# Score tiles in pairs, and O items 13 behind H, in a fused attention and feed-forward kernel

## The chip, the core and the metric

The kernel runs on one core of a Trainium2 chip. The core has a matrix engine (TensorE, PE in the profile, with its weight loads on a row PEld), two engines for elementwise work that can read the matrix results (VectorE, DVE; ScalarE, ACT), one [...] (GpSimd, POOL), and SyncE (SP), which here only issues DMAs. Matrix results land in PSUM, eight banks of 128 x 512 float32. Everything else lives in the on-chip memory or, by DMA, in the chip's main memory. The metric is the time of one execution in microseconds (us).

## What is computed

Attention with a window of 128 keys and a linear position bias over 8 batches, 8 heads, 576 positions and head size 64, then a feed-forward layer over the 4608 tokens that come out of it:

```python
def _attn_ref(q, k, v):                      # 8 x 8 x 576 x 64
    scores = scale * np.matmul(q, k.transpose(0, 1, 3, 2))
    bias = slopes[:, None, None] * (-np.abs(rel))[None, :, :]
    mask = (rel >= 0) & (rel < 128)
    scores = np.where(mask, scores + bias[None], -1000000000.0)
    attn = softmax(scores)
    return np.matmul(attn, v)

def _moe_ref(x, w_in, w_out, beta):          # 4608 x 512, 512 x 2048, 2048 x 512
    h = x @ w_in
    g = h * (1.0 / (1.0 + np.exp(-beta * h)))
    return g @ w_out
```

## The kernel before

*Feed-forward.* The tokens are worked in 9 groups of 512. An H item (`HS(g, j)`, L356) is four matmuls of 128 x 512 into one bank `hps`; ScalarE takes a tanh of it (`sig`, L369) and VectorE makes the gate from both (`gT`, L370), which frees the bank. Two banks serve `hps`, so the H after next waits for the gT of this one. Sixteen H make a group. An O item (`OS(g, i, n)`, L374) is four matmuls (L380) that add a quarter of the sum over the 2048 features to an O tile, one of four tiles of 128 tokens in a group. With n = 3 the tile is done: ScalarE copies it out (`osb`, L395) and a DMA, mostly on POOL's queue, stores it. Two banks serve O tiles.

*Attention.* Queries and keys are loaded on SP's queue (L95), cast by POOL (L129), transposed by a DMA on SP's queue (`TD`, L248) into `QK`; values are loaded by POOL's queue (L137) from batch 3 on. A score tile (`SC(b, m, p)`, L257) holds the two heads of pair p against half the key blocks of batch b: m = 0 the blocks 0 and 1, m = 1 the blocks 2, 4 and 3. It is four or six matmuls (L277) over 64 rows, the two heads on the two halves of the array's rows, each head with a bank of its own. Its tile `sps` is two banks, and there is one such tile. From batch 2 on ScalarE then takes four exponentials (L290), two a head, and VectorE multiplies by a mask (L294), which gives `pt`; for batches 0 and 1 the bias is added by matmuls and there is one exponential. There are 8 score tiles a batch, 40 in batches 3 to 7.
A value item (`PV(b, qb, g)`, L306) is four or eight matmuls of 65 columns for one block of queries and four heads, into one of two banks tagged "t"; VectorE divides by the sum (`zs`, L326, and `xn`, L327). `X(b, qb)` brings xn into the transposed tokens `XT` that H reads: by matmuls and a copy for batches 0 to 2, by a DMA on SP's queue (L341) from batch 3 on.

*Order.* PE's order is written by hand, and around the change so are those of SP and POOL; the framework orders ScalarE and VectorE. From batch 2 on, `moe` lists the H and O items, and `merge(steps, first)` lists the attention's steps with the loads, casts and transposes set among them by step number. `spread(moe, todo, lead, goals)` goes through `moe` and lays the steps between the items, by a cost of 2 for a score tile and 1 for a PV, so that each goal (the tokens of a group, 10 items before its first H) is met. The score tiles thus stand alone, with two to five H and O items between them. O items run 10 behind H: the list `late` (10 items) of one group and `early` (6) of the next go between the H. In `early` two O tiles alternate.

The banks are: `psum_s` 2 (one score tile), `psum_t` 2 (values, transposes), `psum_h` 2, `psum_o` 2.

Of the kernel before, what the change touches and what calls it, by code (L numbers as in the profile page):

```python
# [17 lines left out]
def kernel(  # L18
# [235 lines left out]
    COLS = {0: (0, 384), 1: (128, 256), 2: (0, 384), 3: (192, 320), 4: (128, None)}  # L254
    OWN = (256, 320)

    def SC(b, m, p, pool=None, fill=0):  # L257
        qk = QK[b % 2]
        sps = (pool or psum_s).tile([P, 2, 512], F32, name="sps", tag="sps")
        idle(sps[:, 0, :], fill)  # L260
        if b < NPE:
            for e in range(2):
                nc.tensor.matmul(  # L263
                    sps[:, e, :], lhsT=sident[:, 2 * p + e, :], rhs=table[m][:],
                    start=True, stop=False, skip_group_check=True,
                )
        for kb in ((0, 1), (2, 4, 3))[m]:
            at, after = COLS[kb]
            nq = {3: P + 64, 4: 64}.get(kb, 2 * P)
            for e in range(2):  # L270
                o = sps[:, e, at : at + min(nq, 512 - at)]
                if kb in (0, 2):
                    o = bass.AP(
                        tensor=o.tensor, offset=o.offset,
                        ap=[list(o.ap[0]), [after - at, 2], [1, P]],
                    )
                nc.tensor.matmul(  # L277
                    o,
                    lhsT=qk[64 * e : 64 * e + 64, 1, p, P * kb : P * kb + P],
                    rhs=qk[64 * e : 64 * e + 64, 0, p, P * kb : P * kb + nq],  # L280
                    start=b >= NPE, stop=True, skip_group_check=True,
                )
        pt = pt_pool.tile([P, 2, 512], BF16, name="pt", tag="pt")
        if b < NPE:
            nc.scalar.activation(out=pt[:], in_=sps[:], func=ACTF.Exp, scale=qscale)  # L285
        else:
            for e in range(2):
                h = 2 * p + e
                for half, cols in ((0, slice(0, OWN[m])), (1, slice(OWN[m], 512))):
                    nc.scalar.activation(  # L290
                        out=pt[:, e, cols], in_=sps[:, e, cols], func=ACTF.Exp,
                        scale=qscale, bias=bias[:, half, h : h + 1],
                    )
            nc.vector.tensor_tensor(  # L294
                out=pt[:], in0=pt[:],
                in1=masks[m][:].rearrange("p (o c) -> p o c", o=1).broadcast_to([P, 2, 512]),
                op=ALU.mult,
            )
        pts[b, m, p] = pt
# [166 lines left out]
    def pv(b, qb, g):  # L466
        return step(lambda: PV(b, qb, g), 1)
# [43 lines left out]
    def by_pair(b):  # L511
# [5 lines left out]
            pv(b, 2, 1),  # L517
        ]

    def by_block(b):  # L520

        e = b - 1
        if e < NTE:
            r = [sc(b, 0, 0), pv(e, 3, 1), sc(b, 0, 1), x(e, 3), pv(e, 4, 1)]
        else:
            r = [sc(b, 0, 0), pv(e, 2, 1), x(e, 2), pv(e, 3, 1), x(e, 3), sc(b, 0, 1),
                 pv(e, 4, 1), x(e, 4)]
        return r + [
            sc(b, 0, 2), pv(b, 0, 0)] + ([x(e, 4)] if e < NTE else []) + [
            sc(b, 0, 3), pv(b, 1, 0), sc(b, 1, 0), pv(b, 0, 1), x(b, 0),  # L530
            sc(b, 1, 1), pv(b, 1, 1), x(b, 1), sc(b, 1, 2), pv(b, 2, 0), sc(b, 1, 3), pv(b, 3, 0),
            pv(b, 4, 0),
        ]

    with tc.manual_schedule(engines={mybir.EngineType.PE}):

        for sb in range(NQB):
            c = load_v(0, sb)()
            if sb in (1, 3):
                with tc.issue_after(c.ins):  # L540
                    for n in ((0,), (1, 2))[sb // 2]:
                        load_w1(n)
        for p in range(NP):
            c = load_pair(1, p, None if p else VS[0][0:1, NQB - 1, 0, 0:1])
            if p == 1:
                with tc.issue_after(c.ins):
                    load_w1(3)
                load_tail(1)
        for sb in range(NQB):
            c = load_v(1, sb)()  # L550
            if sb == 3:
                with tc.issue_after(c.ins):
                    for n in range(4):
                        load_w2(n)
        with tc.tile_pool(name="psum_x", bufs=2, space=bass.MemoryType.PSUM) as psum_x:
            pools = [psum_x, psum_s, psum_x]

            def sc0(m, p, fill=0):
                SC(0, m, p, pools[0], fill)
                pools.append(pools.pop(0))  # L560

            w = psum_t.tile([P, 512], F32, name="w", tag="t")
            idle(w[:], 9)
            TP(0, 0, 0)
            c = TP(0, 0, 1)
            with tc.issue_after(c.ins):
                late_consts()
            sc0(0, 0, 3)
            load_beta()
            TP(0, 1, 0)  # L570
            TP(0, 1, 1)
            sc0(0, 1, 2)
            TT(0)
            TP(0, 2, 0)
            sc0(1, 0, 1)
            TP(0, 2, 1)
            sc0(1, 1)
            TP(0, 3, 0)
            sc0(0, 2)
            TP(0, 3, 1)  # L580
            sc0(1, 2)
            PV(0, 0, 0)
            sc0(0, 3)
            PV(0, 1, 0)
            sc0(1, 3)
            for qb in (2, 3):
                PV(0, qb, 0)
        psum_h = ctx.enter_context(
            tc.tile_pool(name="psum_h", bufs=2, space=bass.MemoryType.PSUM))
        def hs(g):  # L590
            return [lambda j=j: HS(g, j) for j in range(NFF)]

        h0, s1 = hs(0), by_pair(1)
        with tc.tile_pool(name="psum_z", bufs=2, space=bass.MemoryType.PSUM) as psum_z:
            spare["z"] = psum_z
            w = psum_s.tile([P, 2, 512], F32, name="w", tag="sps")
            for qb in range(NQB - 1):
                PV(0, qb, 1, (psum_z, "ops") if qb % 2 else (psum_h, "hps"))  # L600
                idle(w[:, 0, :], 1)
                if qb:
                    X(0, qb - 1)
            X(0, NQB - 2)
            for it in [
                h0[0], pv(0, 4, 0), h0[1], pv(0, 4, 1), h0[2], h0[3], x(0, 4), h0[4], h0[5],
                s1[0], h0[6], s1[1],
            ]:
                it()
            del spare["z"]  # L610
        for p in range(NP):
            load_pair(2, p)
            if p == 1:
                load_tail(2)

        with tc.tile_pool(name="psum_y", bufs=1, space=bass.MemoryType.PSUM) as psum_y:
            spare["y"] = [psum_s, psum_y]
            spread(h0[7:14], s1[2:-1], 0, [(7, len(s1) - 3)])
            del spare["y"]
        psum_o = ctx.enter_context(  # L620
            tc.tile_pool(name="psum_o", bufs=2, space=bass.MemoryType.PSUM))
        for it in s1[-1], h0[14], pv(1, 3, 1), x(1, 2), h0[15], x(1, 3):
            it()

        s2 = by_pair(2)
        for f in s2[0:2]:
            f()
        steps, first = [pv(1, 4, 1)] + s2[2:9] + [x(1, 4)] + s2[9:] + [x(2, 2)], {}
        for b in range(NTE, B):
            first[b] = len(steps)  # L630
            steps += by_block(b)
        steps += [pv(B - 1, 2, 1), x(B - 1, 2), pv(B - 1, 3, 1), x(B - 1, 3), pv(B - 1, 4, 1),
                  x(B - 1, 4)]
        with tc.manual_schedule(engines={mybir.EngineType.SP, mybir.EngineType.Pool}):

            early = [(0, 0), (1, 0), (0, 1), (1, 1), (0, 2), (1, 2)]
            late = [(0, 3), (1, 3)] + [(i, n) for i in (2, 3) for n in range(4)]

            def os(g, order):
                return [lambda i=i, n=n: OS(g, i, n) for i, n in order]  # L640

            todo, goals = merge(steps, first), []
            moe = hs(1) + os(0, early + late) + os(1, early)
            for g in range(2, NTG):
                b, r = divmod(TOKG * (g + 1) - 1, S)
                goals.append((len(moe) - 10, todo.index(at[b, r // P]) + 1))
                o = os(g - 1, late) + (os(g, early) if g < NTG - 1 else [])
                h = hs(g)
                moe += sum(([h[n]] + o[n : n + 1] for n in range(NFF)), [])
            spread(moe, todo, 2, goals)  # L650
            while stores:
                flush()
            for it in os(NTG - 1, early + late):
                it()


# [28 lines left out]
```

## Time and profile before

| What | Value |
|---|---|
| Time, median of 6 runs | 335.56 us (333.5 to 338.3) |
| The profiled execution: time, span | 335.34 us, 333.2 us |
| L364 (H), 576 matmuls of 512 columns | 144.1 us busy |
| L380 (O), 576 matmuls of 512 columns | 142.5 us busy |
| L277 (scores), 320 matmuls | 35.7 us busy in three shapes |
| L369 tanh, x144 | 99.1 us on ScalarE, mean 691 ns |
| L290 exponentials, x192 | 75.0 us on ScalarE as a union, mean 478 ns |
| L370 gate, x144; L294 mask, x48 | 98.3 and 35.4 us on VectorE |
| DMA, 100 to 120 us; 220 to 240 us; 260 to 280 us | 187, 80 and 47 GB/s |

A row of the profile's list of groups gives line, engine, operation, what is written from what, and how often; of PE some records are missing (554 of 576 for H). The matmuls are pipelined: one of 512 columns is shown with 379 ns, yet the next begins 216 ns after it, so an item of four takes 0.86 us from its start to the next item's start. In the timeline each line is a run of instructions: start, duration, engine, line, operation, count, and in brackets the engine's idle time before it with what ended it. A row "issue" of the waits is time in which the engine waited for nothing that the profile shows.

### The profile page before, as it was taken

The numbers are of one execution on the slowest core, as the hardware profiler recorded it, in microseconds if no ns is written. First come the engines' busy times: TensorE is split into PE (matmuls) and PEld (weight loads), VectorE is DVE, ScalarE is ACT, GpSimd is POOL, SyncE is SP. The second block draws the span as 40 slices with busy tenths as digits, with TensorE's granted clock in tenths as the row PEclk, the third lists the DMA queues.
The fourth block names the chain that finished last, engine by engine and source line by source line (L and its number), as shares of the span: only waits on it lengthen the run. The fifth ranks groups of instructions, "written<-read, shape, count | busy, mean of one in ns | idle before, by whom it ended". The sixth has DMA issues, their size and how long they took to land.

```text
span 333.2 us, 6160 instructions
## 1 busy us (share of the span) xinstructions
PE 317.5 (95%) x2237; PEld 151.7 (46%) x2280; DVE 192.0 (58%) x413; ACT 215.4 (65%) x416; POOL 106.5 (32%) x173
## 2 busy tenths in 40 slices
PE   8989799999999999999999999999999999999895
PEld 3454345444544444444444444444444444444342
DVE  7658468995336675556566656566565555334500
ACT  5667684896558867777677667775776664454611
POOL 6743582163753525424242334420100010010000
PEclk9999999999999999999999999999999999999999
DMA  7999999999999999999999879990402002010011
GB/s 186 241 195 246 236 228 238 180 192 180 224 220 170 182 192 192 173 174 231 119 223 159 155 112 202 183 137 3 103 31 65 31 33 84 19 65 31 32 62 66
DMA packets 138638, 48.26 MB, mean 145 GB/s; under 512 B 125664, under 2 KB 136176, under 8 KB 138608
## 3 DMA queue, kind: packets, MB, share of 16 engines
q1 hardware_dynamic: 108208, 32.19, 53.3%
q0 software_dynamic: 30224, 15.54, 30.6%
q8 instruction: 18, 0.29, 0.4%
q10 hardware_dynamic: 176, 0.14, 0.1%
q14 instruction: 12, 0.10, 0.1%
HBM read 36.71 MB, written 9.44 MB: 138 GB/s over the span
## 4 chain that ended last, share of the span: by engine, by line
PE 84%; DMA 6%; DVE 3%; SPq 2%; POOL 2%; issue 1%; ACT 1%
PE ops L380 37%; PE hps L364 34%; PE sps L277 5%; DMA fst<-in_k_dram 5%; PE pv L321 3%; PE pv L317 2%; DMA fst<-in_v_dram 2%; SPq L109 1%; DVE gT L370 1%; PE tps L224 1%; ACT sig L369 1%; PE sps L263 1%; DVE xn L327 1%; POOL W L188 1%; DVE pt L294 1%
## 5 line engine op out<-in xcount | busy, mean ns | idle before, releaser
L364 PE MATMUL hps<-XT,W 128*128 128x512 bf16 x554 | 144.1, 379 | 3.4 <-DVE gT L370 1.5
L369 ACT ACTIVATE sig<-hps,beta_h 128x512 bf16<-128x512 f32 x144 | 99.1, 691 | 72.7 <-PE hps L364 66.3
L380 PE MATMUL ops<-W,gT 128*128 128x512 bf16 x558 | 142.5, 379 | 1.2 <-issue 0.3
L370 DVE SCALAR_TENSOR_TENSOR gT<-sig,hps 128x512 bf16<-128x512 bf16 x144 | 98.3, 684 | 56.4 <-ACT sig L369 55.7
L290 ACT ACTIVATE pt<-sps,bias 128x256 bf16<-128x256 f32 (+1 forms) x192 | 75.0, 478 | 11.0 <-PE sps L277 11.0
L364 PEld LDWEIGHTS <-W 128*128 128x128 bf16 x576 | 52.0, 98 | 58.8 <-issue 5.6
L380 PEld LDWEIGHTS <-gT 128*128 128x128 bf16 x576 | 51.2, 97 | 55.7 <-issue 2.1
L294 DVE TENSOR_TENSOR pt<-pt,mask 128x1024 bf16<-128x1024 bf16 x48 | 35.4, 737 | 42.9 <-ACT pt L290 42.9
L398 POOL DMA_DIRECT2D out_dram<-osb x32 | 17.9, 560 | 110.5 <-ACT osb L395 110.5
L129 POOL CAST bst<-fst 128x512 bf16<-128x512 f32 (+1 forms) x50 | 32.0, 644 | 57.8 <-DMA fst<-in_q_dram 37.9
L327 DVE TENSOR_TENSOR xn<-pv,zs 128x256 bf16<-128x256 f32 (+1 forms) x80 | 33.7, 422 | 2.4
L395 ACT ACTIVATE osb<-ops 128x512 f32<-128x512 f32 x35 | 21.0, 601 | 18.1 <-PE ops L380 18.0
L321 PE MATMUL pv<-vs,pt 128*128 128x65 bf16 x320 | 28.7, 193 | 1.5 <-DVE qkT L243 0.5
L321 PEld LDWEIGHTS <-pt 128*128 128x128 bf16 x320 | 21.7, 97 | 11.2 <-DVE qkT L243 0.7
L277 PE MATMUL sps<-qkT 64*128 64x256 bf16 (+2 forms) x320 | 25.2, 252 | 0.1
L317 PE MATMUL pv<-vs,pt 128*128 128x65 bf16 x256 | 24.0, 193 | 0.7 <-DVE XT L350 0.5
L326 DVE RECIPROCAL zs<-pv 128x4 f32<-128x4 f32 (+1 forms) x80 | 14.1, 176 | 16.5 <-PE pv L321 16.2
L317 PEld LDWEIGHTS <-pt 128*128 128x128 bf16 x256 | 19.9, 98 | 7.5 <-issue 1.0
L277 PEld LDWEIGHTS <-qkT 64*128 64x128 bf16 x320 | 10.4, 94 | 27.5 <-issue 24.2
L137 POOL DMA_DIRECT2D vs<-in_v_dram x25 | 21.4, 859 | 1.0 <-issue 0.5
L285 ACT ACTIVATE pt<-sps 128x1024 bf16<-128x1024 f32 x16 | 16.3, 1023 | 6.5 <-PE sps L277 5.8
L113 POOL CAST bst<-fst 128x512 bf16<-128x512 f32 x24 | 14.6, 621 | 18.4 <-DMA fst<-in_q_dram 11.4
(49 smaller groups left out, 109.5 us busy)
## 6 DMA issues: line engine op xcount, KB each, us to landing
fst<-in_q_dram SPq DMA_DIRECT2D x32, 256.0 KB, 4.6
fst<-in_k_dram SPq DMA_DIRECT2D x32, 256.0 KB, 5.1
out_dram<-osb POOLq DMA_DIRECT2D x32, 256.0 KB, 3.1
fst<-in_v_dram SPq DMA_DIRECT2D x12, 256.0 KB, 7.2
vs<-in_v_dram POOLq DMA_DIRECT2D x20, 128.0 KB, 5.5
W<-in_moe_w_in_dram POOLq DMA_DIRECT2D x4, 512.0 KB, 7.2
W<-in_moe_w_out_dram POOLq DMA_DIRECT2D x4, 512.0 KB, 15.3
fst<-in_q_dram SPq DMA_DIRECT2D x8, 128.0 KB, 5.4
```

Of the source, the lines that this page charges most:

```text
L129: nc.gpsimd.tensor_copy(out=t[0 : ROWS[sb], i], in_=f)
L137: nc.gpsimd.dma_start(out=to, in_=v[b, :, P * sb : P * sb + ROWS[sb], :].rearrange("h p d -> p h d"))
L277: nc.tensor.matmul(o, lhsT=qk[64 * e : 64 * e + 64, 1, p, P * kb : P * kb + P], rhs=qk[64 * e : 64 * e + 64, 0, p, P * kb : P * kb + nq], ...
L290: nc.scalar.activation(out=pt[:, e, cols], in_=sps[:, e, cols], func=ACTF.Exp, scale=qscale, bias=bias[:, half, h : h + 1],)
L294: nc.vector.tensor_tensor(out=pt[:], in0=pt[:], in1=masks[m][:].rearrange("p (o c) -> p o c", o=1).broadcast_to([P, 2, 512]), op=ALU.mult,)
L317: nc.tensor.matmul(pv[:, hl, 0 : D + 1], lhsT=weights(b, qb - 1, h, 1), rhs=vs[:, qb - 1, h, 0 : D + 1], start=True, stop=False,)
L321: nc.tensor.matmul(pv[:, hl, 0 : D + 1], lhsT=weights(b, qb, h, 0), rhs=vs[:, qb, h, 0 : D + 1], start=qb == 0, stop=True,)
L327: nc.vector.tensor_tensor(out=xn[0:nq, 4 * g : 4 * g + 4, :], in0=pv[0:nq, :, 0:D], in1=zs[0:nq].broadcast_to([nq, 4, D]), op=ALU.mult,)
L364: nc.tensor.matmul(hps[:], lhsT=W1[:, c, bass.ts(j, P)], rhs=XT[:, c, c0 : c0 + TOKG], start=(c == 0), stop=(c == NDM - 1),)
L369: nc.scalar.activation(out=sig[:], in_=hps[:], func=ACTF.Tanh, scale=beta_h[:, j : j + 1])
L370: nc.vector.scalar_tensor_tensor(out=gts[g][:, j, :], in0=sig[:], scalar=1.0, in1=hps[:], op0=ALU.add, op1=ALU.mult)
L380: nc.tensor.matmul(ops_[:], lhsT=gT[:, j, i * P : i * P + P], rhs=W2[:, j, :], start=(j == 0), stop=(j == NFF - 1),)
```

## The change

- In batches 3 to 7 score tiles are issued two at a time (`visit`). The first keeps the two banks of `psum_s`. The second, `split=True`, has its heads in two single banks: one of the O tiles' pool and one of the value pool.
- A pair stands at the start of each stretch of eight H and O items, between the H that follows an O tile's last item and the next O tile's first. The steps of the batch are cut into stretches at the pairs, and `spread` lays each stretch's steps among its own eight items. Two more stretches without a pair (`pause`) hold the end of batch 7.
- O items run 13 behind H and tile by tile: `early` and `late` are replaced by one order, (0,0), (0,1), (0,2), (0,3), (1,0) and so on. The stretch before the first pair has 28 items, the next two 4 and 6.
- `PV(b, 3, 0)` and `PV(b, 4, 0)` move from the end of their batch behind the first pairs of the next one, and the second halves of block 2 of batch 2 too.

The attention's steps then advance by one batch in 32 items.

```diff
-    def SC(b, m, p, pool=None, fill=0):
+    def SC(b, m, p, pool=None, fill=0, split=False):
         qk = QK[b % 2]
-        sps = (pool or psum_s).tile([P, 2, 512], F32, name="sps", tag="sps")
-        idle(sps[:, 0, :], fill)
+        if split:
+
+            sps = [
+                psum_o.tile([P, 512], F32, name="sps0", tag="ops")[:],
+                psum_t.tile([P, 512], F32, name="sps1", tag="t")[:],
+            ]
+        else:
+            both = (pool or psum_s).tile([P, 2, 512], F32, name="sps", tag="sps")
+            sps = [both[:, e, :] for e in range(2)]
+        idle(sps[0], fill)
...
+    visits = []
+
+    def visit(b, m, p):
+        def f():
+            SC(b, m, p)
+            SC(b, m, p + 1, split=True)
+
+        visits.append(f)
+        return [f, lambda: None]
+
+    def pause():
+        visits.append(lambda: None)
+        return [visits[-1]]
+
     def by_block(b):
 
         e = b - 1
         if e < NTE:
-            r = [sc(b, 0, 0), pv(e, 3, 1), sc(b, 0, 1), x(e, 3), pv(e, 4, 1)]
+            r = [pv(e, 2, 1), pv(e, 3, 1), x(e, 2), x(e, 3)], [pv(e, 4, 1), x(e, 4)]
         else:
-            r = [sc(b, 0, 0), pv(e, 2, 1), x(e, 2), pv(e, 3, 1), x(e, 3), sc(b, 0, 1),
-                 pv(e, 4, 1), x(e, 4)]
-        return r + [
-            sc(b, 0, 2), pv(b, 0, 0)] + ([x(e, 4)] if e < NTE else []) + [
-            sc(b, 0, 3), pv(b, 1, 0), sc(b, 1, 0), pv(b, 0, 1), x(b, 0),
-            sc(b, 1, 1), pv(b, 1, 1), x(b, 1), sc(b, 1, 2), pv(b, 2, 0), sc(b, 1, 3), pv(b, 3, 0),
-            pv(b, 4, 0),
-        ]
+            r = [pv(e, 2, 1), x(e, 2), pv(e, 3, 0), pv(e, 3, 1), x(e, 3)], [
+                pv(e, 4, 0), pv(e, 4, 1), x(e, 4)]
+        return (
+            visit(b, 0, 0) + r[0] + visit(b, 0, 2) + r[1]
+            + visit(b, 1, 0) + [pv(b, 0, 0), pv(b, 0, 1), x(b, 0)]
+            + visit(b, 1, 2) + [pv(b, 1, 0), pv(b, 1, 1), x(b, 1), pv(b, 2, 0)]
+        )
...
-            early = [(0, 0), (1, 0), (0, 1), (1, 1), (0, 2), (1, 2)]
-            late = [(0, 3), (1, 3)] + [(i, n) for i in (2, 3) for n in range(4)]
+
+            order = [(i, n) for i in range(4) for n in range(4)]
...
-            todo, goals = merge(steps, first), []
-            moe = hs(1) + os(0, early + late) + os(1, early)
+            todo = [[]]
+            for f in merge(steps, first):
+                if f in visits:
+                    todo.append([])
+                todo[-1].append(f)
+            moe = [hs(1) + os(0, order[0:12]), os(0, order[12:]), os(1, order[0:3])]
             for g in range(2, NTG):
-                b, r = divmod(TOKG * (g + 1) - 1, S)
-                goals.append((len(moe) - 10, todo.index(at[b, r // P]) + 1))
-                o = os(g - 1, late) + (os(g, early) if g < NTG - 1 else [])
-                h = hs(g)
-                moe += sum(([h[n]] + o[n : n + 1] for n in range(NFF)), [])
-            spread(moe, todo, 2, goals)
+                o = os(g - 1, order[3:]) + (os(g, order[0:3]) if g < NTG - 1 else [])
+                for j, h in enumerate(hs(g)):
+                    moe[-1].append(h)
+                    if j % 4 == 1:
+                        moe.append([])
+                    moe[-1] += o[j : j + 1]
+            for n, m in enumerate(moe):
+                r = todo[n] if n < len(todo) else []
+                if n and r:
+                    r.pop(0)()
+                spread(m, r, 2 if n == 0 else 1, [(len(m) - (n == 0), len(r))])
             while stores:
                 flush()
-            for it in os(NTG - 1, early + late):
+            for it in os(NTG - 1, order):
                 it()
```

More of the change, by code (lines that the diff above doesn't have):

```diff
@@ L263, in SC @@
                 nc.tensor.matmul(
-                    sps[:, e, :], lhsT=sident[:, 2 * p + e, :], rhs=table[m][:],
+                    sps[e], lhsT=sident[:, 2 * p + e, :], rhs=table[m][:],
                     start=True, stop=False, skip_group_check=True,
@@ L270, in SC @@
             for e in range(2):
-                o = sps[:, e, at : at + min(nq, 512 - at)]
+                o = sps[e][:, at : at + min(nq, 512 - at)]
                 if kb in (0, 2):
@@ L284, in SC @@
         if b < NPE:
-            nc.scalar.activation(out=pt[:], in_=sps[:], func=ACTF.Exp, scale=qscale)
+            nc.scalar.activation(out=pt[:], in_=both[:], func=ACTF.Exp, scale=qscale)
         else:
@@ L290, in SC @@
                     nc.scalar.activation(
-                        out=pt[:, e, cols], in_=sps[:, e, cols], func=ACTF.Exp,
+                        out=pt[:, e, cols], in_=sps[e][:, cols], func=ACTF.Exp,
                         scale=qscale, bias=bias[:, half, h : h + 1],
@@ L627 @@
             f()
-        steps, first = [pv(1, 4, 1)] + s2[2:9] + [x(1, 4)] + s2[9:] + [x(2, 2)], {}
+        steps, first = [pv(1, 4, 1)] + s2[2:9] + [x(1, 4)] + s2[9:-1], {}
         for b in range(NTE, B):
@@ L631 @@
             steps += by_block(b)
-        steps += [pv(B - 1, 2, 1), x(B - 1, 2), pv(B - 1, 3, 1), x(B - 1, 3), pv(B - 1, 4, 1),
-                  x(B - 1, 4)]
+        e = B - 1
+        steps += pause() + [pv(e, 2, 1), x(e, 2), pv(e, 3, 0), pv(e, 3, 1), x(e, 3)]
+        steps += pause() + [pv(e, 4, 0), pv(e, 4, 1), x(e, 4)]
         with tc.manual_schedule(engines={mybir.EngineType.SP, mybir.EngineType.Pool}):
-            early = [(0, 0), (1, 0), (0, 1), (1, 1), (0, 2), (1, 2)]
-            late = [(0, 3), (1, 3)] + [(i, n) for i in (2, 3) for n in range(4)]
+            order = [(i, n) for i in range(4) for n in range(4)]
             def os(g, order):
                 return [lambda i=i, n=n: OS(g, i, n) for i, n in order]
-            todo, goals = merge(steps, first), []
-            moe = hs(1) + os(0, early + late) + os(1, early)
-            for g in range(2, NTG):
-                b, r = divmod(TOKG * (g + 1) - 1, S)
-                goals.append((len(moe) - 10, todo.index(at[b, r // P]) + 1))
-                o = os(g - 1, late) + (os(g, early) if g < NTG - 1 else [])
-                h = hs(g)
-                moe += sum(([h[n]] + o[n : n + 1] for n in range(NFF)), [])
-            spread(moe, todo, 2, goals)
+            todo = [[]]
[4 more added lines that the diff above has]
+            moe = [hs(1) + os(0, order[0:12]), os(0, order[12:]), os(1, order[0:3])]
+            for g in range(2, NTG):
+                o = os(g - 1, order[3:]) + (os(g, order[0:3]) if g < NTG - 1 else [])
[9 more added lines that the diff above has]
+                spread(m, r, 2 if n == 0 else 1, [(len(m) - (n == 0), len(r))])
             while stores:
                 flush()
-            for it in os(NTG - 1, early + late):
+            for it in os(NTG - 1, order):
                 it()
```

## The prediction

> **What bounds the kernel now.** I read the busy table and the 40 slices first, then the waits, the timeline around one score tile, SP's queue and the end.
>
> ```profile
> PE 317.5 (95%) x2237; PEld 151.7 (46%) x2280; DVE 192.0 (58%) x413; ACT 215.4 (65%) x416; POOL 106.5 (32%) x173
> ...
> PE   8989799999999999999999999999999999999895
> ...
> DMA  7999999999999999999999879990402002010011
> ```
>
> TensorE is the bound from the sixth slice to the end; only what takes time out of its row counts. The waits of TensorE (first row: its weight loads) show where it loses any:
>
> ```profile
> PEld L277 <- issue: 24.2, 57, 0.4
> ...
> PE hps L364 <- DVE gT L370: 1.5, 2, 0.9
> ```
>
> 57 score tiles each begin with 0.4 us in which no weights are loaded, and twice an H waits for VectorE. The timeline shows both. A score tile of batch 5, m = 1:
>
> ```profile
> 172.76 1.03 PE L364 MATMUL hps<-XT,W 128*128 128x512 bf16 x4
> ...
> 173.72 0.39 PE L277 MATMUL sps<-qkT 64*128 64x256 bf16 x6
> 173.82 0.69 ACT L369 ACTIVATE sig<-hps,beta_h 128x512 bf16<-128x512 f32 x1 [1.04 <-PE hps L364]
> ...
> 174.05 1.04 PE L380 MATMUL ops<-W,gT 128*128 128x512 bf16 x4
> ...
> 174.41 1.56 ACT L290 ACTIVATE pt<-sps,bias 128x320 bf16<-128x320 f32 x4
> ...
> 174.92 1.03 PE L364 MATMUL hps<-XT,W 128*128 128x512 bf16 x4
> ...
> 175.98 0.69 ACT L369 ACTIVATE sig<-hps,beta_h 128x512 bf16<-128x512 f32 x1
> 176.00 0.69 DVE L294 TENSOR_TENSOR pt<-pt,mask 128x1024 bf16<-128x1024 bf16 x1 [0.77 <-ACT pt L290]
> ...
> 176.61 0.17 DVE L326 RECIPROCAL zs<-pv 128x4 f32<-128x4 f32 x1
> ```
>
> Elsewhere an H or O item follows the last after 0.86 us (175.91 to 176.77), so the scores could begin at 173.62; they begin at 173.72. They stream 0.23 us and O begins at 174.05, not 173.95; its successor comes after 0.87, not 0.86. A visit to the 64-row mode thus costs 0.10 + 0.09 + 0.01 = 0.20 us beside its streaming.
>
> **The change part by part.** The sum is made against the profiled execution: 335.34 us, span 333.2 and 2.1 around it, 0.2 under the median of 335.56.
>
> *Pairs.* 40 lone tiles become 20 pairs: 20 x 0.20 = 4.0 us less on TensorE, the path. Inside a tile a second set of weights costs 0.01 beyond streaming; 20 of those at the seams give back 0.2. The trace has no seam between two tiles in different banks; bounds are 0 and the whole 0.20 (nothing gained); I take 0.01, since the nearest rows, the second keys of a tile, have the same row halves and no lone drain. Gain 3.8. The Trainium skill (TensorE: Matmul & The Clock Gate, section Single matmul latency) puts the drain of a matmul that nothing follows at roughly 175 ns; with that at each change of mode, two a pair, the gain would be 20 x 0.35 = 7.0. The row's 0.10 and 0.09 are measured here, and I keep them.
>
> *The end.* Group 8, the last, now has 13 O items among its 16 H, not 10. Before, six H in a row have two hps banks, and each bank comes back 1.6 us after its H:
>
> ```profile
> 311.02 1.89 PE L364 MATMUL hps<-XT,W 128*128 128x512 bf16 x8 [0.85 <-DVE gT L370]
> ...
> 313.54 0.81 PE L364 MATMUL hps<-XT,W 128*128 128x512 bf16 x3 [0.64 <-DVE gT L370]
> ```
>
> Counted from start to start the two gaps are 1.0 and 0.8. Now three H stand together; only the third waits: 0.8. Gain 1.0. The last stores are unchanged, since the last two O tiles ran one by one before too.
>
> *The burst.* A pair issues eight exponentials at once, and the tanh of the next H stands behind them on ScalarE's queue; that H's bank is wanted by the second H after it. Times from the end of streaming of the H ahead of the pair: that H's tanh runs from 0.20 (173.62 to 173.82) and lets the next start at 0.79 (174.41); eight exponentials occupy to 0.79 + 2 x 1.57 = 3.93 for m = 1 (174.41 to 175.98 each tile), 3.65 for m = 0 (1.43 each). The next H's tanh, ready at 2.6, ends at 4.62 (4.34). On VectorE the second mask is ready at 3.95 (3.80), the zs and xn of the first PV at 3.6; the mask spaces the row by 0.61 (176.00 to 176.61), zs by 0.21, xn by 0.34, gT takes 0.68 and frees the bank 0.06 later. Meanwhile TensorE does: pair to 0.66, O 0.87, H, O, PV (0.13 or 0.24), H, O (0.86 each), in two of four pairs a second PV, then the H that wants the bank: at 5.11 after pair (1,0), written (m, first p), 5.23 after (0,2), 5.47 after (0,0) and (1,2).
> With zs, xn, mask, gT in this order for m = 1 the bank is free at 5.48 and 5.60: waits of 0.36 and 0.13; for m = 0, with the mask ahead of xn, at 5.25: about 0. Sum 0.5 a batch, 2.5 us in five. VectorE's queue isn't written out by hand, so its order is unknown: with the mask first and gT next, 0.27 a batch at the least (1.4 in all); with gT last of the four, 0.73 + 0.38 + 0.47 + 0.23 = 1.8 a batch, 9 in all. I take 2.5: at 176.00 and 176.61 the trace has mask and zs in the order in which they became ready.
> The skill speaks against the change here: TensorEngine Tiling (Array Packing), section PSUM Bottleneck, says that tiling speeds up TensorE but not the emptying of PSUM, which may become the bottleneck. By sums it doesn't: eight items and a pair take some 8.1 us of TensorE (8 x 0.86 + 0.66 + 2.5 PV), ScalarE 3.0 + 4 x 0.69 + 0.60 = 6.4. It holds only locally, as worked out.
>
> *The new banks.* The first half tile takes the O bank that the last pair left; its eight exponentials ended 4 us ago. The O tile after the pair takes the bank of the tile that ended; an H and the pair (1.5 us) cover its 0.6 us copy. Twice in batch 3 no H lies between: 0.2 each. The value bank is free for as long. These banks cost nothing while that H stands there; without it, 0.2 a pair, 4 us.
>
> *Start, and moved DMAs.* Batches 3 to 7 take some 32.5 us each now (29 to 37 before, by the tile starts 89.5, 118.6, 154.5, 192.1, 228.8), and batch 3 comes sooner. Its 10 loads, 10 key and query transposes and 5 or 6 value transposes stand on SP's queue, which has no gap from 66 to 157 us:
>
> ```profile
> 93.39 0.76 SPq L95 DMA_DIRECT2D fst<-in_k_dram  x1
> 94.26 6.20 SPq L248 DMA_TRANSPOSE qkT<-bst  x4
> 100.52 0.58 SPq L95 DMA_DIRECT2D fst<-in_q_dram  x1
> ```
>
> The second of the four, batch 3's last, is issued at 96.45 and lands 4.3 later, at 100.8. Its scores began at 104.6; now, by counting items, at about 98.3 (first pair at 87.0 and 11.3 of items): up to 2.5 us of waiting, less what earlier loads in the new list win. I take 1.5, with 0 and 3 as ends; the O waits above and a wait of the first pair for the transposes of 82.9 (landing 5.1 later) lie within it. After that a batch needs some 32 us of SP (118.8 to 151.0 from first load to first load, without a gap) against 32.5 of TensorE: just covered. POOL's casts, value loads and stores take 14 us a batch, and all keep their order; X comes 16 us or more ahead of its H but for group 3, where some 1 us is left. PV, O and H are as many as before.
>
> Sum: 335.3 - 3.8 - 1.0 + 2.5 + 1.5 = 334.5, that is 1.1 under the median.
>
> **The rivals.**
> *The cover holds* (TensorE gets the pairs whole): the burst costs 0 to 1 and the start 0 to 1. 335.3 - 4.8 + 0.5 = 331.0. For it: ScalarE at 65%, and PV counts that I took at their least. Against: the 0.3 that pair (1,0) lacks in any order.
> *The burst decides, slower*: gT placed last after each pair, 9 us: 335.3 - 4.8 + 9 + 1.5 = 341.0. It turns the sign above 3.3 us, 0.17 a pair. For it: at 177.16 gT does stand behind zs and xn though its tanh was done at 176.67. Against: there the hps bank wasn't late.
> *SP becomes the bound*: 85.5 to 118.8, loads of batch 4 to loads of batch 5, took SP 33.3 us; with 34 a batch over four, less 3 us of lead, 3 more: 337.5.
> *No drain saved*: TensorE drains between the two tiles as well: 335.3 - 1.0 + 2.5 + 1.5 = 338.3. Nothing in the trace shows it.
>
> **How the numbers follow.** Central case 0.45 (its own range 332.4 to 336.5), cover 0.30, burst 0.12, SP 0.08, no drain 0.05. What a measurement of this kernel can tell from no change is about 1%, here 332.2 to 338.9. Faster: most of the cover case and the low edge of the central one, 0.32. Slower: most of the burst, a part of SP and of no drain, 0.17. Same: 0.51. Range: 330.5 (cover whole) to 338.9, leaving out the worst of the burst.
>
> **What would show it.** The wait of weight loads for L277 should fall from 57 to some 37 times; pairs of eight or twelve score matmuls with 0.23 us a tile and no gap between. "hps waits for gT" should grow from 1.5 to about 3 us, at the third H after a pair, most where m = 1. A wait of some 1 us before the third pair of batch 3, for a transpose. In the end a single wait of 0.8. I am wrong if that first row keeps its count, if the hps waits are near zero or above 6 us, or if TensorE waits for transposes in batches 5 to 7.

## The result and the profile after

The changed kernel takes 332.56 us (median of 18 runs, 330.63 to 335.58) against 335.65 (39 runs of the kernel before): a ratio of 0.9906, interval 0.9882 to 0.9931. That is 3.1 us less. The forecast was 334.5, with 330.5 to 338.9 as its range: the direction is right and the value lies inside the range, but the gain is nearly three times the 1.1 us forecast, mainly because one cost in the sum, that of the burst of exponentials, hardly came.

The page of the changed kernel's profiled execution (333.95 us, so 1.4 over its median), its span, busy table and slices:

```profile
span 332.1 us, 6155 instructions
...
PE 315.2 (95%) x2238; PEld 153.6 (46%) x2280; DVE 191.2 (58%) x413; ACT 214.7 (65%) x416; POOL 107.3 (32%) x173
...
PE   7979798999998998999999999999999999999995
...
PEclk9999799999999999999999999999999999999999
DMA  7999999999999999998999999921122200001011
```

TensorE is still the bound, at the same share. DMA's busy stretch ends sooner (its last slice with a 9 is the 26th, not the 27th), since the attention is done sooner: the last scores begin at 240.1 us, not 257.9. One slice, 33.2 to 41.5 us, has a mean granted clock of 0.79, ahead of everything that was changed. My estimate of its cost is 0.21 x 8.3 = 1.7 us; the kernel before has 1.00 there. That it explains the 1.4 over the median isn't shown: another profile of the same kernel has no such slice and took 333.44.

The granted clock matters for the comparison: at 0.997 and above the kernel before takes 334.7 us (median of 32 runs; only runs whose clock is on record are taken) and at 0.995 and below 337.0 (20 runs), the changed one 332.2 (15) and 332.6 (18), so the gain is 2.4 or 4.3 us and the 3.1 lies between.

The waits, of the weight loads and of TensorE, scores and H only (engine and line, who was waited for, us in total, times, longest):

```profile
PEld L285 <- issue: 14.6, 35, 0.4
```

```profile
PE hps L372 <- DVE gT L378: 1.8, 2, 1.2
...
PE sps L285 <- DMA qkT<-bst: 0.8, 1, 0.8
```

The wait of the last H of all, in the timeline:

```profile
313.29 1.02 PE L372 MATMUL hps<-XT,W 128*128 128x512 bf16 x4 [0.64 <-DVE gT L378]
```

The first row answers to 57 times and 24.2 us: 22 fewer, for 20 pairs (a few records are missing in either). The second, 1.5 before, hides two things: 0.6 is the last H of all (0.8 from start to start), and 1.2 is a wait for a transpose of tokens, shown below with SP's order. The timeline of a pair with m = 1, first p = 2, batch 5:

```profile
174.11 1.02 PE L372 MATMUL hps<-XT,W 128*128 128x512 bf16 x4
...
175.06 0.61 PE L285 MATMUL sps<-qkT 64*128 64x256 bf16 x12
175.17 0.69 ACT L377 ACTIVATE sig<-hps,beta_h 128x512 bf16<-128x512 f32 x1 [0.39 <-PE hps L372]
175.61 1.04 PE L388 MATMUL ops<-W,gT 128*128 128x512 bf16 x3
175.75 3.02 ACT L298 ACTIVATE pt<-sps,bias 128x320 bf16<-128x320 f32 x8
...
178.60 0.75 ACT L377 ACTIVATE sig<-hps,beta_h 128x512 bf16<-128x512 f32 x1
178.80 0.69 DVE L302 TENSOR_TENSOR pt<-pt,mask 128x1024 bf16<-128x1024 bf16 x1 [0.76 <-ACT pt L298]
...
179.41 0.68 DVE L378 SCALAR_TENSOR_TENSOR gT<-sig,hps 128x512 bf16<-128x512 bf16 x1
...
180.01 0.18 DVE L334 RECIPROCAL zs<-pv 128x4 f32<-128x4 f32 x1
```

Twelve score matmuls follow each other without a gap: from their first start to O's start it is 0.55 us, twice the 0.23 of a tile and 0.09 for the return. Streaming of the H ahead ends at 174.97 (174.11 + 0.86). The eight exponentials start at 175.75 and the tanh of the next H at 178.60, that is 0.79 and 3.63 after it; its gT follows the mask at once, and zs and xn come last. The gate is done at 180.09 (179.41 + 0.68), 5.12 after that end of streaming, and the H that wants the bank starts at 180.43 here, without a wait. Only after pair (1,0), where it is due sooner, does it wait: 0.08 us, as the starts of the matmuls show (once a batch, in batches 4 to 7; in batch 3 that pair itself was late).

From the first score tile of batch 2 to the last matmul the kernel before takes 269.5 us (59.3 to 328.9), the changed one 266.7 (61.0 to 327.7). Ahead of that tile nothing of the order on TensorE was changed; three profiles of the changed kernel have it at 61.0, 61.6 and 59.9, so that part varies by 1.7 us by itself. The 2.8 us within, by the starts of the matmuls: pairs -4.2 (0.21 each), the end -1.0 (one wait of 0.8, not two of 1.0 and 0.8), a wait of 0.7 in batch 2 gone (a value item, PV, waited for its mask); and more: 1.5 in waits in the stretches of the first three pairs of batch 3, 1.3 ahead of the first H of group 3, 0.3 for the burst. That makes -2.8. The wait that went is in the kernel before:

```profile
PE pv L321 <- DVE pt L294: 0.5, 1, 0.5
```

The 2.8 is of one profile of each kernel. The other two profiles of the changed kernel have 265.6 us (start at 61.6) and 267.4 (start at 59.9) for the same stretch. The sooner TensorE comes to batch 3, the longer it waits there for transposes: 0.6 and 0.8 us from 61.6, 1.0 and 1.3 from 61.0, 1.9 and 1.4 from 59.9. So the last matmul begins at 327.3, 327.7 and 327.3, whatever the start was; this fits the small difference that the clock makes to the changed kernel.

### The profile page after: what moved, and what is told of

Same layout as the page of the kernel before. It is cut to its first block, busy times and chain, and to the rows that moved or that the text cites. A ratio compares the mean times of both kernels' runs of the same rounds, so it can differ in the third digit from the quotient of the medians.

```text
span 332.1 us, 6155 instructions
## 1 busy us (share of the span) xinstructions
PE 315.2 (95%) x2238; PEld 153.6 (46%) x2280; DVE 191.2 (58%) x413; ACT 214.7 (65%) x416; POOL 107.3 (32%) x173
## 4 chain that ended last, share of the span: by engine, by line
PE 65%; DMA 22%; SPq 5%; POOL 2%; ACT 2%; DVE 1%; issue 1%; POOLq 0%
PE ops L388 32%; PE hps L372 27%; DMA fst<-in_k_dram 10%; DMA fst<-in_q_dram 6%; DMA fst<-in_v_dram 6%; PE sps L285 3%; PE pv L329 2%; SPq L248 2%; SPq L109 2%; SPq L95 1%; PE pv L325 1%; DMA qkT<-bst 1%; POOL bst L129 1%; ACT pt L298 1%; DVE gT L378 1%
## 5 line engine op out<-in xcount | busy, mean ns | idle before, releaser
L377 ACT ACTIVATE sig<-hps,beta_h 128x512 bf16<-128x512 f32 x144 | 99.8, 696 | 81.9 <-PE hps L372 62.1
L388 PEld LDWEIGHTS <-gT 128*128 128x128 bf16 x576 | 53.8, 98 | 64.1 <-issue 2.1
L372 PEld LDWEIGHTS <-W 128*128 128x128 bf16 x576 | 51.2, 98 | 53.7 <-issue 4.7
L298 ACT ACTIVATE pt<-sps,bias 128x256 bf16<-128x256 f32 (+1 forms) x192 | 72.9, 492 | 3.2 <-PE sps L285 3.2
L129 POOL CAST bst<-fst 128x512 bf16<-128x512 f32 (+1 forms) x50 | 33.0, 660 | 77.7 <-DMA fst<-in_q_dram 59.3
L302 DVE TENSOR_TENSOR pt<-pt,mask 128x1024 bf16<-128x1024 bf16 x48 | 34.1, 710 | 35.5 <-ACT pt L298 35.4
L285 PE MATMUL sps<-qkT 64*128 64x256 bf16 (+2 forms) x320 | 22.2, 252 | 1.0 <-DMA qkT<-bst 0.8
L285 PEld LDWEIGHTS <-qkT 64*128 64x128 bf16 x320 | 11.2, 94 | 20.6 <-issue 14.6
```

The lines of the kernel that those rows point to most:

```text
L129: nc.gpsimd.tensor_copy(out=t[0 : ROWS[sb], i], in_=f)
L285: nc.tensor.matmul(o, lhsT=qk[64 * e : 64 * e + 64, 1, p, P * kb : P * kb + P], rhs=qk[64 * e : 64 * e + 64, 0, p, P * kb : P * kb + nq], ...
L298: nc.scalar.activation(out=pt[:, e, cols], in_=sps[e][:, cols], func=ACTF.Exp, scale=qscale, bias=bias[:, half, h : h + 1],)
L302: nc.vector.tensor_tensor(out=pt[:], in0=pt[:], in1=masks[m][:].rearrange("p (o c) -> p o c", o=1).broadcast_to([P, 2, 512]), op=ALU.mult,)
L372: nc.tensor.matmul(hps[:], lhsT=W1[:, c, bass.ts(j, P)], rhs=XT[:, c, c0 : c0 + TOKG], start=(c == 0), stop=(c == NDM - 1),)
L377: nc.scalar.activation(out=sig[:], in_=hps[:], func=ACTF.Tanh, scale=beta_h[:, j : j + 1])
```

## The experiments

Three questions: is it the pairs that bring the gain; why was the burst of exponentials nearly free, and on what does that hang; and are the new waits in batch 3 SP's order?

**Pairs taken apart.** The second tile of a pair comes one O item later.

```diff
         def f():
             SC(b, m, p)
-            SC(b, m, p + 1, split=True)
 
         visits.append(f)
-        return [f, lambda: None]
+        return [f, lambda: SC(b, m, p + 1, split=True)]
```

> The changed kernel, but with one O item between the two score tiles of a pair, so that TensorE changes its row mode four times a stretch, not two. Banks, ScalarE's and VectorE's order stay. Theory (what pairs bring is the change of mode, 0.19 us each visit): 20 x 0.19 = 3.8 us more than the changed kernel, about 336.4, level with before; the lone weight-load waits of the scores go from 35 to about 55. Rival (the gain comes from the new order of O and from the end, pairs bring nothing): 332.6, unchanged.

Measured: 335.92 us, ratio to before 0.9996 (0.996 to 1.0031): by the medians the gain is gone. The weight loads' waits:

```profile
PEld L285 <- issue: 23.7, 56, 0.4
```

From the first pair of batch 4 to that of batch 7 this kernel takes 99.8 us, and the starts of its matmuls show no wait of TensorE there; the changed one takes 98.8 with 1.5 us of waits in it, so 97.3 without. For 12 pairs that is 0.21 us each. Taking apart also shortens the waits in batch 3 (0.6 us in its pairs and none ahead of group 3, where the changed kernel has 1.5 and 1.3), since TensorE comes later to the same transposes: a part of what pairs bring is given back there. So not all of the gain hangs on the pairs. From batch 2's first score tile to the last matmul this kernel takes 268.5 us, 1.8 over the changed one and 1.0 under the kernel before. The times agree with this once the clock is the same: 334.1 us (4 runs at 0.997 and above) and 336.0 (8 below) are 0.5 and 1.0 under the kernel before and 1.9 and 3.4 over the changed one.

**The new order of O alone.** The kernel before with O tile by tile, 13 behind H:

```diff
-            early = [(0, 0), (1, 0), (0, 1), (1, 1), (0, 2), (1, 2)]
-            late = [(0, 3), (1, 3)] + [(i, n) for i in (2, 3) for n in range(4)]
+            order = [(i, n) for i in range(4) for n in range(4)]
+            early, late = order[0:3], order[3:]
```

> The kernel before with one part of the change: O items tile by tile and 13 behind H, score tiles alone as before. Theory: the last group has 13 O items among its H, so of the two waits of an H for a gate at the end (1.0 and 0.8) one remains, of 0.8: 1.0 us less than before, 334.6. Rival (the order of O is worth the whole difference): 332.6. A second rival: tile by tile makes an O tile wait for its bank's copy and costs some 0.2 us a tile, 36 tiles, 7 us more.

Measured: 335.12 us, ratio 1.0002 (0.9973 to 1.0032): not the 1.0 less that I expected. The end is as expected, one wait of 0.8 us. But in batch 2 TensorE waits 1.8 us in all (0.6 for a PV, 0.8 and 0.4 where tokens or keys are transposed) where before waits 0.7: what the end gains, these waits give back. Why they grew wasn't tested. So the order of O alone doesn't make the kernel faster; in the changed kernel its 1.0 at the end counts, since these waits in batch 2 don't come there, and it makes room for the pairs. No O tile waits for its bank: the second rival falls too.

**A longer burst.** Two of each pair's exponentials are done twice, with the same values:

```diff
-            for e in range(2):
+            for e in (0, 1, 1) if split else (0, 1):
```

> The changed kernel with two exponentials of every pair done twice (the same values again), so that ScalarE's burst has ten, not eight. Theory (the tanh of the next H stands behind the burst, and the second H after it wants its bank; the cover is short by 0.08 in pair (1,0) and long by 0.1 to 0.4 in the others): 0.71 us more in the queue gives waits of about 0.8, 0.6, 0.35 and 0.35 in a batch, 2.1 a batch, 10 us in all: 343. Rival (ScalarE at 65% has room, a burst of any such size is absorbed): 332.6, and no wait of an H.

Measured: 342.61 us, ratio to before 1.0214 (1.0147 to 1.0281). The timeline of a pair (1,0):

```profile
175.92 1.34 ACT L377 ACTIVATE sig<-hps,beta_h 128x512 bf16<-128x512 f32 x2
176.14 0.69 DVE L302 TENSOR_TENSOR pt<-pt,mask 128x1024 bf16<-128x1024 bf16 x1 [0.36 <-ACT pt L298]
176.75 1.28 DVE L378 SCALAR_TENSOR_TENSOR gT<-sig,hps 128x512 bf16<-128x512 bf16 x2
177.48 1.02 PE L372 MATMUL hps<-XT,W 128*128 128x512 bf16 x4 [0.65 <-DVE gT L378]
```

H waits for gT, which waits for the tanh behind the burst. From start to start the wait is 0.82 here; it is 0.71 after (0,2) and 0.46 after the other two: 2.4 us a batch. The chain of the prediction is right, then; the real burst exceeds its cover by less than 0.1 us after one pair in four and stays inside it after the others. ScalarE at 65% has no room at this place.

**The pair one item earlier**, behind the O item that ends a tile and ahead of the H:

```diff
                     moe[-1].append(h)
-                    if j % 4 == 1:
-                        moe.append([])
                     moe[-1] += o[j : j + 1]
+                    if j % 4 == 0:
+                        moe.append([])
```

> The changed kernel with each pair one item earlier: directly behind the O item that ends a tile, ahead of the H. Theory (the H ahead of the pair is what makes the burst nearly free, since its tanh runs before the exponentials and the next H comes later): the tanh of the H behind the pair now waits for all eight exponentials, to 3.6 us after the pair's start, its bank is free at 5.15, and the H that wants it is due at 4.3: 0.85 us a pair, 17 us in all, 349. Rival (placing within a stretch doesn't matter): 332.6. A second rival (only the copy of the ended O tile counts, and an H still stands ahead of the next O tile): 332.6 to 334.

Measured: 345.77 us, ratio 1.0312 (1.025 to 1.0374). A pair and what follows it:

```profile
170.46 0.61 PE L285 MATMUL sps<-qkT 64*128 64x256 bf16 x12
...
171.06 3.02 ACT L298 ACTIVATE pt<-sps,bias 128x320 bf16<-128x320 f32 x8
...
173.92 1.33 ACT L377 ACTIVATE sig<-hps,beta_h 128x512 bf16<-128x512 f32 x2
174.12 0.69 DVE L302 TENSOR_TENSOR pt<-pt,mask 128x1024 bf16<-128x1024 bf16 x1 [0.77 <-ACT pt L298]
174.73 1.28 DVE L378 SCALAR_TENSOR_TENSOR gT<-sig,hps 128x512 bf16<-128x512 bf16 x2
175.46 1.02 PE L372 MATMUL hps<-XT,W 128*128 128x512 bf16 x4 [0.69 <-DVE gT L378]
```

The tanh starts at nearly the same distance from the pair's start (3.46 us, 3.54 in the changed kernel), but the H that wants the bank is due an item sooner. There are 18 such waits, all but one between 0.70 and 0.86 us by the starts, near the 0.85 expected; they make 14 us, not 17: the first two pairs of batch 3 have no such wait, and the mean is 0.79. One place in the list decides between 3 us gained and 10 lost.

**SP's order in batch 3.** The two waits of the changed kernel first. Its third pair of batch 3, and the first H of group 3 with the transpose that it reads (SPq is SP's queue):

```profile
99.92 0.28 PE L285 MATMUL sps<-qkT 64*128 64x256 bf16 x2
101.03 0.34 PEld L285 LDWEIGHTS <-qkT 64*128 64x128 bf16 x10 [1.02 <-DMA qkT<-bst]
```

```profile
127.52 1.85 SPq L349 DMA_TRANSPOSE XT<-xn  x1
...
129.56 1.03 PE L388 MATMUL ops<-W,gT 128*128 128x512 bf16 x3
129.66 0.68 DVE L378 SCALAR_TENSOR_TENSOR gT<-sig,hps 128x512 bf16<-128x512 bf16 x1
...
130.80 0.67 DVE L378 SCALAR_TENSOR_TENSOR gT<-sig,hps 128x512 bf16<-128x512 bf16 x1
131.75 1.02 PE L372 MATMUL hps<-XT,W 128*128 128x512 bf16 x4 [1.17 <-DVE gT L378]
```

The pair stands for 1.0 us between its first key block and the next. The H's wait is put down to a gate. But H items use two banks by turns, and the bank that this H wants came free with the gate of 129.66, at 130.34; the one of 130.80 is for the H after it. The transpose issued at 127.52 landed 4.1 us later (the view of DMA issues), at 131.6, and the H follows. That is the 1.2 in the row of waits. The edit moves DMA issues alone:

```diff
-                jobs.append((t0, lambda b=b, sb=sb, c=casts: c.append(load_qk(b, sb))))
+                d = {(NTE + 1, 1): 1.5, (NTE + 2, 1): 0.5}.get((b, sb), 0)
+                jobs.append((t0 + d, lambda b=b, sb=sb, c=casts: c.append(load_qk(b, sb))))
...
-                jobs.append((i + 2, f))
+                jobs.append((i, f))
```

The changed kernel was timed beside it.

> The changed kernel itself, for comparison on the same chip: 332.6 (331.5 to 333.5) for every theory; 35 lone weight-load waits of the scores, and waits of TensorE of about 1.0 us in the third pair of batch 3 and about 1.3 us ahead of the first H of group 3.

> The changed kernel with three things moved on SP's queue alone: the loads of batch 4, block 1, behind the last transposes of batch 3; the loads of batch 5, block 1, behind the transpose of batch 3's tokens that the first H of group 3 reads; and every transpose of tokens asked for two steps earlier. Theory (the two waits of TensorE in batch 3 are the queue's order: each transpose stands behind loads that nobody needs yet): both waits go, 1.0 + 1.3 us, 330.3. Rival (the queue's total work is the bound from 66 to 150 us, so what moves ahead makes something else late): the two waits go and others of the same size come, in the pairs of batches 4 and 5; 332.6.

Measured: 331.31 us for the changed kernel beside it (0.6 and 0.8 us in the two waits), 330.41 for this one (ratios to before 0.9871 and 0.9843, with intervals that overlap widely). The times can't tell 1 us apart; the profile can. The same pair and the same H:

```profile
99.78 0.44 PEld L285 LDWEIGHTS <-qkT 64*128 64x128 bf16 x12 [0.42 <-issue]
99.79 0.61 PE L285 MATMUL sps<-qkT 64*128 64x256 bf16 x12
```

```profile
PE hps L372 <- DVE gT L378: 0.6, 1, 0.6
```

All twelve scores run together, the only wait of an H for a gate is the last of all, and no wait of the rival's kind comes in batches 4 and 5. From batch 2's first score tile to the last matmul it takes 264.5 us against 265.6 in the profile beside it.

One profile without these waits doesn't prove the edit, though. The next kernel below (last H alone) has SP's order as in the changed kernel, and in its profile the first wait is missing and the second is 0.2:

```profile
100.74 0.61 PE L285 MATMUL sps<-qkT 64*128 64x256 bf16 x12
```

There TensorE came to batch 2 late, at 62.0, and the last key or query transpose of batch 3 landed at 99.5, 1.2 us ahead of its pair. In the three profiles of the changed kernel it landed 0.7 to 1.9 us after the pair's start. What speaks for the edit is where it puts that transpose: it lands at 97.6 here, 2.2 us ahead of the pair, and 3.3 and 2.3 ahead in the two profiles of the version with both edits below. None of these three has either wait, though TensorE comes to batch 2 at 60.9, 58.5 and 59.1 in them.

**The last H, and both.** The last H is given a bank of the values' pool:

```diff
+        if g == NTG - 1 and j == NFF - 1:
+            pool, tag = psum_t, "t"
         if j % 2 and (g == 1 and j < NFF - 1 or "z" in spare):
```

> The changed kernel with the very last H in a bank of the values' pool, which is empty by then, so that it doesn't wait for a gate. Theory: the last wait of 0.8 us goes, 331.8. Rival (the end is bound by the gates of the last H, which O then waits for): the wait moves to the O item that reads the last gates, 332.6.

> Both of the last two together. Theory: 332.6 - 2.3 - 0.8 = 329.5. Rival (the waits in batch 3 come back elsewhere): 331.8.

Measured: 330.75 us for the last H alone and 329.31 for both. In the profile of both together the last wait (0.8 from start to start) is gone, and the O items follow the last three H directly:

```profile
306.87 2.75 PE L374 MATMUL hps<-XT,W 128*128 128x512 bf16 x12
309.46 1.89 PE L390 MATMUL ops<-W,gT 128*128 128x512 bf16 x8
```

Timed once more, beside the changed kernel:

> The changed kernel again, beside the next one on one chip: 331.3 to 332.6.

> The version with SP's queue reordered in batch 3 and the last H in a bank of the values' pool, again, timed more often: if its gain over the changed kernel is the three waits (1.4 to 2.3 us in batch 3, 0.8 at the end), 2.2 to 3.1 us under the changed kernel of the same call. If the first timing owed its lead to the varying start, less than 1.

Measured: 332.18 us (ratio to before 0.990, 0.9866 to 0.9934) and 330.30 (0.986, 0.9805 to 0.9915). The lead is 1.9 us, a little under the 2.2 expected; the intervals overlap, so the size isn't settled by times. In that pair of profiles the stretch from batch 2's first score tile takes 267.4 and 263.7 us, with starts at 59.9 and 59.1. It is the fastest version tried, 1.4% under the kernel before.

## Why the prediction was right, and where it was off

- *Pairs, -3.8.* Right, a little small: 0.21 a pair, 4.2 in all, as the pairs taken apart show. The seam between two tiles costs nothing at all, where I had allowed 0.01. The estimate with a longer drain, 0.35 a pair and 7.0 in all, is refuted; so is the rival in which nothing is saved.
- *The end, -1.0.* Right: one wait of 0.8 in place of 1.8. That O's order alone brings nothing, because waits in batch 2 take the 1.0 back, wasn't foreseen; nor that in the changed kernel the 0.7 of wait there would go.
- *The burst, +2.5.* The chain was right, as the longer burst and the earlier pair show, and its size wrong: 0.3. By the sign that the prediction itself set (waits of H for its gate near zero) this term failed, and the rival *The cover holds* was right here. Two of its parts were off. I took 1.57 us for the four exponentials of a tile with m = 1, from 174.41 to the tanh at 175.98; but that tanh was waiting for its own H, and the tile alone occupies ScalarE for 1.42. The next tanh thus starts at 3.63, not 3.93. And I let zs and xn stand ahead of the mask, while the order has gT straight behind the mask. With both put right (mask at 3.84, gT 0.61 later at 4.44, 0.68 long, 0.06 to the release) the same sum has the bank free at 5.18 where H comes at 5.11, 5.23, 5.47 and 5.47: 0.07 a batch; 0.08 was measured. This sum was made after the result, from the changed kernel's trace.
- *The start, +1.5.* Right, for the reason given: the transposes of batch 3's last block land after the pair is due. In the profile where TensorE comes to batch 2 nearly as in the kernel before (59.9, not 59.3), the third pair comes at 98.57, where 98.3 was counted. That the profile has just 1.5 in these stretches is luck: of the third pair's wait it has 1.0, two other profiles of the same kernel 1.9 and 0.6.
- *Group 3.* The prediction saw 1 us left and put no cost there; the profile has 1.3 us of wait, 0.8 and 1.4 in two others. A margin of 1 us was too thin for a queue on which the transposes of tokens take from 2.4 to 7.3 us to land in this profile.
- *SP as the bound* in later batches: not seen. After batch 3 the changed kernel's scores wait for no transpose.

The miss of 1.9 us is thus 2.2 from the burst, 0.4 from the pairs and 0.7 from the wait in batch 2 that went, less 1.3 in group 3; that makes 2.0, for one profile of each kernel. The waits in batch 3 differ by more than a microsecond between profiles, so the split is no finer than that. In the overall figure two misses, the burst and group 3, work against each other.

## What to carry to other kernels

If a matrix engine is the bound, collect its short visits to another row mode: here the price, 0.2 us, was paid for each visit, not for each tile. What such a group sends to the next engine comes as one burst; place it behind the last item whose result the other engine must serve first, and count when the item queued behind the burst is needed, since the average load of that engine (65% here) says nothing about it. And before the gain of a faster stretch is counted, look for a queue that it will run into: here the transposes of batch 3 took up to 3.2 us of it back. A duration read as the distance between two starts is only an engine's time if the second start waited for nothing else.

## What the runs showed of the hardware

The change to 64 rows and back costs 0.096 and 0.093 us, with another 0.01 between the first matmul after it and the second, nearly the same at every visit of every profile here, and two tiles in four different banks follow each other without a gap.

Unexpected was how much the stretch ahead of the changed part varies: 56.3 to 62.0 us over these profiles (56.3 is the kernel with O's new order alone, in which one H of 0.86 us stands behind the mark), 1.7 us among three of the same kernel. It goes with the granted clock: the five profiles with a slice of seven or eight tenths near 40 us have 61.0 to 62.0, the seven without have 60.9 or less. It is larger than most effects studied here, which is why the starts of matmuls after it were compared, and not the times alone; but where a queue runs at its own pace, as SP's does in batch 3, what comes after isn't independent of it.
